# Late attention over two heads at a time, on two halves of TensorE's rows

## The chip, the core and the metric

One core of one Trainium2 chip runs the whole program. Its engines are TensorE (PE in the profile; PEld is its weight load), VectorE (DVE), ScalarE (ACT), GpSimd (POOL) and SyncE (SP, which here issues every DMA). The metric is the device time of one execution in microseconds (us). Times are compared by the median of several runs.

## The reference

Causal attention with a position bias over 4 batches, 8 heads, 576 positions and head size 64, then two feed-forward layers over the 2304 tokens. In short:

```python
scores = q @ k.T / sqrt(64) + minimum(-(cum[q] - cum[k]), 0)   # cum: running sum of max(s, 0); -1e9 where k > q
attn = softmax(scores);  x = attn @ v                          # the heads side by side: [2304, 512]
h = x @ w_in;   x = (h * clip(h + 3, 0, 6) / 6) @ w_out        # d_ff = 2048
h = x @ w2_in;  y = (h * tanh(softplus(h))) @ w2_out
```

All inputs are float32.

## The kernel before, in words

**Order.** Every step (a DMA, a group of matmuls, one DVE or ACT instruction) is a node with an engine, a cost and a priority. A planner (class `Plan`) runs the nodes through a list schedule when the program is built and writes each engine's instructions in that order. Buffers have tags with a fixed number of slots (`NBUF`), and the slots of a tag are handed out strictly in the order of the nodes' priorities (`turn`): a later user doesn't get a slot before an earlier one has taken his. PSUM has eight banks; late attention has banks 6 and 7, layer one's first matmul 4 and 5, its second 0 to 3.

**Precision.** Operands of the big matmuls are split in a high part (rounded to a shorter float32 format, "fp32r") and a low part (the rest). A product is made of high x high, high x low and low x high.

**Stages.** The queries of a batch are split at 256. *Early* attention (`small`, queries 0 to 255, two heads per call, scores in plain float32 on 64 rows of the array per head) runs first. *Late* attention (`unit`, queries 256 to 575 against all 576 keys) follows and lies among the matmuls of the first layer, since tokens are ordered so that blocks 0 and 1 need only early attention and blocks 2 to 4 the late one. Layer one takes five blocks of tokens (four of 512, one of 256) through 16 steps each: 12 matmuls into a hidden bank (L752), an activation, 12 matmuls with w_out into four banks (L785). At a block's end `y_out` copies the four banks to `st` buffers, ACT or DVE by choice of the planner, and the next block's first w_out matmul needs bank 0 empty. Layer two does the same with its own weights (L752, L790). Weights come in as 64-bit words and are turned into float32 by five DVE or ACT steps each (`load_split`).

**Late attention of one head** (`unit` before): q and k are loaded twice, once into each half of the 128 partitions (`qkr`), copied to the high part (`qk`), and the low parts are made (q's in `ql`, k's in partitions 64 to 127 of `qk`), so that one matmul on 128 rows gives q x (k high + k low). Three tiles of queries (128, 128 and 64) against 384, 512 and 576 keys give scores in banks (L493; the 576 in two halves of 288). DVE adds the bias and finds the row's extreme (L504), ACT takes the exponential (L515), the rows are scaled (L536, L538), PE transposes them 128 columns at a time (L548), ACT and DVE evict high and low part into `pt` (L279, L568), and ten matmuls with `v` (L586) give the head's output, which goes through an `st` buffer to memory (`xs`). A pair of heads shares one `st` buffer; its slot is taken with the first head's L586. `y_out` takes its slots from the same tag, and by priority block 0's come after those of the sixth pair of late attention.

Of the kernel before, what the change touches and what calls it, by code (L numbers as in the profile page):

```python
# [234 lines left out]
def tile_attention_moe_moe(ctx, tc, qk1, qk, v1, s, w_in, w_out, w2_in, w2_out, out):  # L235
    nc = tc.nc

    def r(ap):
# [181 lines left out]

    def unit(b, h, G, ta, tb, pair, prio, step, dep0, depc, banks, fi):
        q0, nk = P * ta, min(S, P * tb)
        nq = nk - q0
        nx = nq + nk
        c0 = COFF[ta]
        cn = (COFF[tb] if tb < 5 else CTOT) - c0
# [515 lines left out]
```

## Time and profile before

| | |
|---|---|
| median of 3 runs | 1042.32 us (1038.67 to 1042.41) |
| the profiled execution | 1043.16 us, its span from first to last instruction 1041.4 us |
| PE busy | 1008.0 us, 97% of the span |
| DVE, ACT, POOL busy | 636.7, 556.2 and 56.1 us |
| granted TensorE clock, mean | 0.981 of full speed |
| late scores (L493), first to last start | 119.6 to 474.9 us |

Matmuls are pipelined, so that a matmul's shown duration is longer than the time by which it delays the next; where this document gives the cost of a group on PE, it is the distance from its start to the next group's start.

### The profile page before, as it was taken

To read this page: it belongs to the slowest core of one execution; us is meant where nothing else is said; L and a number is where in the kernel's file an instruction comes from. 1 tells how busy PE (TensorE), PEld (TensorE's weight loads), DVE (VectorE), ACT (ScalarE), POOL (GpSimd) and SP (SyncE) were. 2 spreads that over 40 slices of the span, in tenths; PEclk is the share of its full clock that TensorE was granted. 3 is DMA by queue.
4 is the path that set the end of the run, shared out by engine and by line. 5 is a ranking of instruction groups with operands and counts; after the bars stand their busy time and mean duration, and the time that the engine had idled before them with its cause. 6 is when DMAs were issued, how large, how long until landed. Compare 5 with 4: busy or idle time off the path is not lost.

```text
span 1041.4 us, 14807 instructions
## 1 busy us (share of the span) xinstructions
PE 1008.0 (97%) x5064; PEld 821.7 (79%) x5064; DVE 636.7 (61%) x1519; ACT 556.2 (53%) x1172; POOL 56.1 (5%) x166
## 2 busy tenths in 40 slices
PE   6889999989999999999999999999999999999998
PEld 3456767867888889998888888888888898888886
DVE  6889999998897889996978999411111212111111
ACT  4878777776787778885435446322322323223222
POOL 2110111001001111000000000000000000000000
PEclk9869999989999999999999999999999999999999
DMA  7786876654645557543435545100100201001001
GB/s 234 232 259 217 310 245 220 213 163 164 219 155 194 163 196 241 198 134 124 154 125 172 172 164 192 59 1 21 41 1 1 81 1 61 1 1 41 1 0 41
DMA packets 60619, 135.63 MB, mean 130 GB/s; under 512 B 7072, under 2 KB 21440, under 8 KB 60544
## 3 DMA queue, kind: packets, MB, share of 16 engines
q1 hardware_dynamic: 60544, 134.69, 38.9%
q8 instruction: 40, 0.66, 0.3%
q14 instruction: 35, 0.29, 0.1%
HBM read 116.07 MB, written 18.59 MB: 129 GB/s over the span
## 4 chain that ended last, share of the span: by engine, by line
PE 82%; DVE 7%; DMA 6%; ACT 2%; issue 2%; SPq 0%; POOL 0%; DVEq 0%; ACTq 0%; POOLq 0%
PE b L752 34%; PE b L790 19%; PE b L785 15%; PE b L493 3%; PE b L548 3%; PE b L586 3%; DMA vr<-in_v_dram 2%; DMA wraw<-in_w_out_dram 2%; PE b L646 1%; PE b L702 1%; DVE cb L504 1%; PE b L693 1%; DVE wtmp L345 1%; DVE qk L444 1%; DMA wraw<-in_w_in_dram 1%
## 5 line engine op out<-in xcount | busy, mean ns | idle before, releaser
L752 PE MATMUL b<-blk,win 128*128 128x512 f32 (+1 forms) x1920 | 500.0, 373 | 2.6 <-DVE e L765 2.6
L752 PEld LDWEIGHTS b<-blk,win 128*128 128x128 f32 x1920 | 341.4, 189 | 67.0 <-DVE e L765 4.7
L785 PE MATMUL b<-g,wo 128*128 128x512 f32 (+1 forms) x960 | 255.4, 376 | 0.5 <-DVE wo L362 0.3
L785 PEld LDWEIGHTS b<-g,wo 128*128 128x128 f32 x960 | 167.2, 188 | 29.0 <-issue 0.8
L770 ACT ACTIVATE e<-b 128x512 f32<-128x512 f32 (+1 forms) x80 | 44.4, 555 | 258.0 <-PE b L752 257.7
L773 DVE TENSOR_TENSOR g<-e,g 128x512 fp32r<-128x512 f32 (+1 forms) x120 | 76.5, 638 | 167.4 <-ACT g L279 167.3
L790 PE MATMUL b<-wo,wo 128*128 128x512 f32 x432 | 121.1, 390 | 0.0
L790 PE MATMUL b<-wo,g 128*128 128x512 f32 x432 | 121.1, 390 | 0.0
L773 DVE TENSOR_TENSOR wo<-e,wo 128x512 fp32r<-128x512 f32 (+1 forms) x40 | 25.5, 638 | 148.2 <-ACT wo L279 148.0
L790 PEld LDWEIGHTS b<-wo,g 128*128 128x128 f32 x432 | 79.9, 188 | 15.5
L790 PEld LDWEIGHTS b<-wo,wo 128*128 128x128 f32 x432 | 79.8, 188 | 15.4
L279 ACT ACTIVATE g<-e 128x512 fp32r<-128x512 f32 (+1 forms) x107 | 63.4, 592 | 36.8 <-DVE e L765 20.1
L515 ACT ACTIVATE cb<-cb,nm 128x512 f32<-128x512 f32 (+2 forms) x96 | 66.9, 697 | 15.7 <-DVE nm L504 15.4
L279 ACT ACTIVATE pt<-b 128x512 fp32r<-128x512 f32 (+2 forms) x128 | 63.0, 497 | 17.0 <-PE b L548 9.6
L763 ACT ACTIVATE e<-b,three 128x512 f32<-128x512 f32 (+1 forms) x80 | 51.1, 639 | 20.5 <-PE b L752 17.6
L504 DVE CUSTOM_DVE_ANT_0 cb<-b,cb 128x512 f32<-128x512 f32 (+2 forms) x96 | 53.6, 562 | 9.3 <-PE b L493 5.9
L568 DVE TENSOR_TENSOR pt<-b,pt 128x320 fp32r<-128x320 f32 (+2 forms) x96 | 54.7, 573 | 4.6 <-ACT pt L279 4.0
L548 PEld LDWEIGHTS b<-ident,cb 128*128 128x128 f32 (+1 forms) x384 | 39.2, 140 | 21.3 <-issue 12.3
L548 PE MATMUL b<-ident,cb 128*128 128x128 f32 (+1 forms) x384 | 52.4, 258 | 2.9 <-DVE nm L504 1.1
L765 DVE SCALAR_TENSOR_TENSOR e<-e,b 128x512 f32<-128x512 f32 (+1 forms) x80 | 50.2, 627 | 2.1 <-ACT e L763 1.9
L586 PEld LDWEIGHTS b<-pt,v 128*128 128x128 f32 x320 | 47.1, 193 | 3.7 <-DVE pt L568 1.7
L369 DVE TENSOR_TENSOR wo<-wo 128x512 fp32r<-128x512 f32 x64 | 44.0, 687 | 8.8 <-ACT wo L279 8.5
(86 smaller groups left out, 1098.5 us busy)
## 6 DMA issues: line engine op xcount, KB each, us to landing
cb<-cuml SPq DMA_DIRECT2D x32, 736.0 KB, 4.5
wraw<-in_w_in_dram SPq DMA_DIRECT2D x32, 512.0 KB, 4.2
wraw<-in_w_out_dram SPq DMA_DIRECT2D x32, 512.0 KB, 4.0
wo<-wos SPq DMA_DIRECT2D x64, 256.0 KB, 3.0
qkr<-in_qk_dram SPq DMA_DIRECT2D x32, 448.0 KB, 3.5
vr<-in_v_dram SPq DMA_DIRECT2D x32, 160.0 KB, 2.5
cb<-cums SPq DMA_DIRECT2D x12, 384.0 KB, 4.8
qkr<-in_qk_dram SPq DMA_DIRECT2D x16, 256.0 KB, 3.1
```

The source lines that it names most:

```text
L279: nc.scalar.activation(out=out_, in_=in_, func=AF.Copy)
L504: nc.vector.tensor_tensor_reduce(out=p.t[0:n, g, o:o + w], in0=ps.t[0:n, z:z + w], in1=cb.t[0:n, g, o:o + w], scale=-0.125, scalar=(3.0e38 ...
L515: nc.scalar.activation(out=p.t[0:n, g, o:o + w], in_=p.t[0:n, g, o:o + w], func=AF.Exp, scale=-1.0, bias=nm.t[0:n, g, k:k + 1], accum_out= ...
L548: nc.tensor.transpose(out=ps.t[:, z:z + n], in_=p.t[0:n, g, o:o + P], identity=ident[0:n, 0:n])
L568: nc.vector.tensor_tensor(out=dl, in0=s_, in1=r(dh), op=ALU.subtract)
L586: nc.tensor.matmul(out=po.t[:, z + a:z + nq], lhsT=vt.t[:, g, c, :], rhs=pt.t[:, mt, g, f:f + nq - a], start=(j == 0), stop=(j == len(todo ...
L752: nc.tensor.matmul(out=hps.t[:, 0:N], lhsT=w.t[:, a, P * c:P * (c + 1)], rhs=x.t[:, c, b, :], start=(c == 0 and k == 0), stop=(c == NCC - ...
L763: a = add("ACT", actp(N, 1), lambda: nc.scalar.activation(out=e0.t[:, 0:N], in_=hps.t[:, 0:N], func=AF.Relu, bias=three, scale=1.0), [prev ...
L765: a = add("DVE", v1x(N), lambda: nc.vector.scalar_tensor_tensor(out=e0.t[:, 0:N], in0=e0.t[:, 0:N], scalar=6.0, in1=hps.t[:, 0:N], op0=ALU ...
L773: gl = add("DVE", v1x(N), lambda: nc.vector.tensor_tensor(out=g.t[:, 1, 0:N], in0=src.t[:, 0:N], in1=r(g.t[:, 0, 0:N]), op=ALU.subtract), ...
L785: nc.tensor.matmul(out=y[j].t[:, 0:N], lhsT=wt.t[:, a, P * j:P * (j + 1)], rhs=g.t[:, b, 0:N], start=(f == 0 and k == 0), stop=(f == NF - ...
L790: nc.tensor.matmul(out=y[j].t, lhsT=g.t[:, a, P * j:P * (j + 1)], rhs=wt.t[:, b, :], start=(f == 0 and k == 0), stop=(f == NF - 1 and k == 2),
```

## The change

`unit` works on two heads at a time. q and k of the pair are loaded once, head 0 in partitions 0 to 63 and head 1 in 64 to 127. The first two tiles of queries are scored per head on 64 rows of the array, three matmuls each (high x high, high x low, low x high), the heads alternating and each in its own bank; a job takes both attention banks at once, for which `can` now counts banks. The last 64 queries of both heads stand side by side as one tile of 128 (zeros fill the other head's rows), scored on all 128 rows and reduced, exponentiated and scaled together. Transposes are therefore all of 128 rows, in six groups per pair. Most buffers now hold a pair: `qk`, `qkr`, `cb`, `nm` and `l` have two slots, `v` and `pt` one. Early attention keeps its V and its transposed probabilities in a `qk` slot instead of `vr` and `pt`. The points at which transposes and products become due are moved.

```diff
     def can(self, n):
         need = {}
+        got = set()
         for b in n.new:
             if isinstance(b, Bank):
-                if not any(k in self.free_banks for k in b.banks):
+                k = next((k for k in b.banks if k in self.free_banks and k not in got), None)
+                if k is None:
                     return False
+                got.add(k)
...
-        "wo": 3, "qk": 2, "qkr": 2, "ql": 2, "cb": 3, "nm": 3, "l": 3, "v": 2, "vr": 1, "pt": 2,
+        "wo": 3, "qk": 2, "cb": 2, "nm": 2, "l": 2, "v": 1, "pt": 1, "qkr": 2,
...
+    def unit(b, h, prio, step, dep0, depc, banks):
+        ta, tb = 2, 5
...
+        nk0 = 3 * P
+        nx = nk0 + nk
...
-        raw = Buf(ap, "qkr", [P, G, nx], F32)
-        t = Buf(ap, "qk", [P, G, nx], F32R)
-        ql = Buf(ap, "ql", [P, G, nq], F32R)
-        cb = Buf(ap, "cb", [P, G, cn], F32)
+        raw = Buf(ap, "qkr", [P, nx], F32)
+        t = Buf(ap, "qk", [P, 2, nx], F32R)
+        cb = Buf(ap, "cb", [P, 2368], F32)
...
-        half, post = prio + 0.713 * step, prio + 1.539 * step
...
-        n_ql = A("DVE", v1x(G * nq), lambda: nc.vector.tensor_tensor(
-            out=ql.t, in0=raw.t[:, :, 0:nq], in1=r(t.t[:, :, 0:nq]), op=ALU.subtract), [n_h], pre, [ql], [raw, t])
-        n_kl = A("DVE", v1x(G * nk), lambda: nc.vector.tensor_tensor(
-            out=t.t[64:P, :, nq:], in0=raw.t[64:P, :, nq:], in1=r(t.t[64:P, :, nq:]), op=ALU.subtract), [n_h], pre, (), [raw, t])
...
+        half, post = prio + 1.0 * step, prio + 2.3 * step
+        n_ld = A("SP", 0.5, lambda: nc.sync.dma_start(out=raw.t, in_=qk[b, h // 2]), dep0, pre, [raw], lat=dma(P * nx * 4))
+
+        def ld_cb():
+            nc.sync.dma_start(out=cb.t[:, 0:1792].rearrange("p (g c) -> p g c", g=2),
+                              in_=cuml[row:row + 2, 0:896].rearrange("(o g) c -> o g c", o=1).to_broadcast([P, 2, 896]))
+            for g in range(2):
+                nc.sync.dma_start(out=cb.t[D * g:D * (g + 1), 1792:2368], in_=cuml[row + g:row + g + 1, 896:1472].to_broadcast([D, S]))
+        n_cb = A("SP", 1.0, ld_cb, depc, pre, [cb], lat=dma(P * 2368 * 4))
+        n_h = A(("ACT", "DVE"), (act(nx), v2x(nx)), lambda e: copy(e, t.t[:, 0, :], raw.t), [n_ld], pre, [t], [raw])
+        n_l = A("DVE", v1x(nx), lambda: nc.vector.tensor_tensor(
+            out=t.t[:, 1, :], in0=raw.t, in1=r(t.t)[:, 0, :], op=ALU.subtract), [n_h], pre, (), [raw, t])
...
+            for s_ in (slice(0, D), slice(D, P)):
+                nc.gpsimd.tensor_tensor(out=cb.t[s_, 2304:2368], in0=cb.t[s_, 2304:2368],
+                                        in1=cmask[s_, P + s_.start:P + s_.stop], op=ALU.add)
+        n_m = A("POOL", 0.9, mask, [n_cb], pre, (), [cb])
+
+        vt = Buf(ap, "v", [P, 2, tb, 2, D], F32R)
...
+        vr = Buf(ap, "qkr", [P, 2, tb, D], F32)
...
-            jobs = [[(i, 0, CW[i])] for i in range(ta, min(tb, 4))]
-            jobs += [[(4, 0, S // 2)], [(4, S // 2, S)]] if tb == 5 else []
-            last_m = None
-            for job in jobs:
-                ps = Bank(banks)
...
-                        for first, m in ((True, t), (False, ql)):
-                            nc.tensor.matmul(out=ps.t[0:n, z:z + e - a], lhsT=m.t[:, g, qo:qo + n], rhs=t.t[:, g, nq + a:nq + e],
-                                             start=first, stop=not first)
...
+        TERMS = ((0, 0), (0, 1), (1, 0))
...
+        for i, a, e in ((2, 0, 384), (3, 0, 512), (4, 0, 288), (4, 288, 576)):
+            w, qo, last = e - a, P * i - q0, e == CW[i]
+            ps = [Bank(banks)] if i == 4 else [Bank(banks), Bank(banks)]
+
+            def mm(ps=ps, i=i, a=a, e=e, w=w, qo=qo):
+                for k, (ka, kb) in enumerate(TERMS):
+                    for g in range(len(ps)):
+                        s_ = slice(0, P) if i == 4 else slice(D * g, D * (g + 1))
+                        nc.tensor.matmul(out=ps[g].t[:, 0:w], lhsT=t.t[s_, ka, qo:qo + P], rhs=t.t[s_, kb, nk0 + a:nk0 + e],
+                                         start=k == 0, stop=k == 2)
+            prev_s = A("PE", 3 * mm_cost(w), mm, [n_h, n_l, n_m, prev_s], prio, ps if prev_s else [*ps, nm, l], [t])
+            for g in range(len(ps)):
...
-        pt = Buf(ap, "pt", [P, 2, G, 1344], F32R)
+        pt = Buf(ap, "pt", [P, 2, 2, 1280], F32R)
...
-                        nc.tensor.transpose(out=ps.t[:, z:z + n], in_=p.t[0:n, g, o:o + P], identity=ident[0:n, 0:n])
-                        z += n
...
+            for g, cs in ([(0, (4, 3)), (0, (2, 1, 0))] if i == 4 else [(0, range(i, -1, -1)), (1, range(i, -1, -1))]):
                 ps = Bank(banks)
-                parts = [(c, i) for c in range(max(tiles) + 1) for i in tiles if c <= i]
-                parts.reverse()
-
-                def tr(ps=ps, parts=parts, g=g):
-                    z = 0
-                    for c, i in parts:
-                        n, o = min(P, S - P * i), COFF[i] - c0 + (P * c if c < 4 else S - P)
-                        nc.tensor.transpose(out=ps.t[:, z:z + n], in_=p.t[0:n, g, o:o + P], identity=ident[0:n, 0:n])
-                        z += n
-                prev_t = A("PE", sum(min(P, S - P * i) for _, i in parts) * 0.0008475, tr, n_n + [prev_t], half, [ps] if prev_t else [ps, pt], [p])
-
-                def views(ps, parts, g):
-                    i = parts[0][1]
-                    n, qo, nch = min(P, S - P * i), P * i - q0, len(parts)
+                nch = len(cs)
+
+                def tr(ps=ps, cs=cs, i=i, g=g):
+                    for z, c in enumerate(cs):
+                        o = off(i, g) + (P * c if c < 4 else S - P)
+                        nc.tensor.transpose(out=ps.t[:, P * z:P * (z + 1)], in_=p.t[:, o:o + P], identity=ident)
+                prev_t = A("PE", nch * P * 0.0008475, tr, [n_n[g], prev_t], half, [ps] if prev_t else [ps, pt], [p])
...
-        v = Buf(ap, "vr", [P, 2, 2, D], F32)
+        v = Buf(ap, "qk", [P, 4 * D + 768], F32)
...
-                unit(b, h, G, ta, tb, pair, prio + h * step, G * step, [n0], [nc0], banks, fi)
+                unit(b, h, prio + h * step, step, [n0], [nc0], banks)
...
-    qk = np.concatenate([qk, qk], axis=2)
+    qk = qk.reshape(NB, NH // 2, P, 320 + S)
+    tail = np.zeros((NB, NH // 2, 2, D, 2, D), np.float32)
+    for g in range(2):
+        tail[:, :, g, :, g] = qk[:, :, D * g:D * (g + 1), 256:320]
+    qk = np.concatenate([qk[..., :256], tail.reshape(NB, NH // 2, P, P), qk[..., 320:]], axis=3)
```

**PE, one unit's scores.** In the kernel before, the eight matmuls of one head, in a stretch where they stand close (b6, b7 are banks; `qk` holds the high q and both parts of k, `ql` the low q):

```order
L493 MATMUL b7_2488<-qk_2449 128x384
L493 MATMUL b7_2488<-qk_2449,ql_2469 128x384
L493 MATMUL b6_2499<-qk_2449 128x512
L493 MATMUL b6_2499<-qk_2449,ql_2469 128x512
...
L493 MATMUL b6_2513<-qk_2449 64x288
L493 MATMUL b6_2513<-qk_2449,ql_2469 64x288
...
L493 MATMUL b6_2527<-qk_2449 64x288
L493 MATMUL b6_2527<-qk_2449,ql_2469 64x288
```
In the changed kernel, the first pair's: the first three of six matmuls of 384 columns, which alternate between the banks, the first two of six of 512, and the two halves of the shared tile.

```order
L493 MATMUL b6_1480<-qk_1425 128x384
L493 MATMUL b7_1481<-qk_1425 128x384
L493 MATMUL b6_1480<-qk_1425 128x384
...
L493 MATMUL b6_1538<-qk_1425 128x512
L493 MATMUL b7_1539<-qk_1425 128x512
...
L493 MATMUL b6_1565<-qk_1425 128x288 x3
...
L493 MATMUL b7_1577<-qk_1425 128x288 x3
```
Sixteen matmuls per pair of heads have become eighteen, twelve of them on 64 rows.

**PE, ahead of block 1's first w_out matmul (into b0).** Before, one row from each group from the last main matmuls (L752, L785) on; L548 are transposes, L493 scores, L586 products with V:

```order
L752 MATMUL b5_2952<-blk_1370,win_626 128x512 x6
L548 MATMUL b6_2982<-ident_69,cb_2733 128x128 x3
L493 MATMUL b7_2987<-qk_2757 128x512
...
L752 MATMUL b5_2952<-blk_1370,win_626 128x512 x3
L548 MATMUL b7_3000<-ident_69,cb_2733 128x128 x4
L493 MATMUL b6_3005<-qk_2757 64x288
...
L548 MATMUL b6_3013<-ident_69,cb_2733 128x64 x5
L493 MATMUL b7_3024<-qk_2757 64x288
...
L586 MATMUL b6_3034<-pt_2983,v_2939 128x320 x6
...
L493 MATMUL b7_3053<-qk_2921 128x384
...
L785 MATMUL b0_3059<-g_2668,wo_2606 128x512 x3
```
Changed (L734 and L767 are the main matmuls, L539 transposes, L493 scores, L577 products):

```order
L734 MATMUL b5_2614<-blk_1231,win_580 128x512 x3
...
L539 MATMUL b7_2647<-ident_69,cb_2273 128x128 x4
...
L539 MATMUL b6_2668<-ident_69,cb_2273 128x128 x3
L577 MATMUL b7_2682<-pt_2622,v_2618 128x320 x6
...
L577 MATMUL b6_2694<-pt_2622,v_2618 128x320 x6
...
L493 MATMUL b6_2721<-qk_2465 128x512
...
L493 MATMUL b6_2748<-qk_2661 128x384
...
L493 MATMUL b6_2767<-qk_2661 128x512
...
L539 MATMUL b6_2785<-ident_69,cb_2493 128x128 x3
...
L539 MATMUL b7_2819<-ident_69,cb_2493 128x128 x3
...
L577 MATMUL b6_2839<-pt_2786,v_2708 128x320 x6
...
L767 MATMUL b0_2860<-g_2387,wo_2291 128x512 x3
```
Between the last L752 or L734 and the first w_out matmul into b0 stand two groups of transposes, four half scores, one head's products and a 384-wide score before; after the change it is ten groups of transposes, three score jobs of both heads, four halves of the shared tile and three heads' products. In both, eleven heads have had products by then.

**ACT, at block 0's output copies (`st` from b0, b1).** Before:

```order
L279 ACTIVATE pt_2983<-b6_2982 128x3x128
...
L279 ACTIVATE pt_2983<-b7_3000 128x4x128
...
L279 ACTIVATE pt_2983<-b6_3013 128x5x64
...
L808 ACTIVATE st_3046<-b0_1089 128x512
...
L808 ACTIVATE st_3057<-b1_1095 128x512
L593 ACTIVATE st_3035<-b6_3034 64x320
```
Changed (L282 is the copy that evicts transposes, L581 a head's output, L790 the output copy of a block):

```order
L282 ACTIVATE pt_2622<-b7_2647 128x4x128
...
L282 ACTIVATE pt_2622<-b6_2668 128x3x2x64
L581 ACTIVATE st_2683<-b7_2682 64x320
L581 ACTIVATE st_2683<-b6_2694 64x320
...
L282 ACTIVATE pt_2786<-b6_2785 128x3x128
...
L282 ACTIVATE pt_2786<-b7_2819 128x3x2x64
L790 ACTIVATE st_2851<-b0_1088 128x512
L790 ACTIVATE st_2854<-b1_1098 128x512
...
L581 ACTIVATE st_2840<-b6_2839 64x320
```
In both, the copy out of b0 stands behind the evictions of the sixth pair's transposes.

## Rows read from the trace of the kernel before

**Rows 1.** The page: the span, the engines' busy time, DVE over forty slices.
```profile
span 1041.4 us, 14807 instructions
...
PE 1008.0 (97%) x5064; PEld 821.7 (79%) x5064; DVE 636.7 (61%) x1519; ACT 556.2 (53%) x1172; POOL 56.1 (5%) x166
...
DVE  6889999998897889996978999411111212111111
```

**Rows 2.** Windows: busy us (and instructions) of each engine, PEclk, DMA share, GB/s.
```profile
78.00:234.00 156.00, 147.69 (x746) 111.59 (x746) 145.90 (x374) 121.23 (x276) 16.17 (x48) 0.98 0.68 229
...
286.00:468.00 182.00, 181.29 (x1173) 159.27 (x1172) 162.39 (x420) 146.80 (x314) 21.34 (x67) 1.00 0.56 183
```

**Rows 3.** Timeline of PE, 284 to 290 us: start, duration, line, tiles, count.
```profile
284.22 1.40 PE L586 MATMUL b<-pt,v 128*128 128x320 f32 x10
285.46 0.42 PE L493 MATMUL b<-qk 128*128 128x384 f32 x1
285.71 0.34 PE L493 MATMUL b<-qk,ql 128*128 128x384 f32 x1
285.89 0.85 PE L785 MATMUL b<-g,wo 128*128 128x512 f32 x3
...
287.95 0.49 PE L548 MATMUL b<-ident,cb 128*128 128x128 f32 x3
288.20 0.48 PE L493 MATMUL b<-qk 128*128 128x512 f32 x1
288.51 0.39 PE L493 MATMUL b<-qk,ql 128*128 128x512 f32 x1
288.74 0.86 PE L785 MATMUL b<-g,wo 128*128 128x512 f32 x3
```

**Rows 4.** Timeline of PE, 404 to 412 us.
```profile
406.04 0.52 PE L752 MATMUL b<-blk,win 128*128 128x256 f32 x3
406.40 0.60 PE L548 MATMUL b<-ident,cb 128*128 128x128 f32 x4
406.75 0.61 PE L785 MATMUL b<-g,wo 128*128 128x256 f32 x3
407.20 0.87 PE L752 MATMUL b<-blk,win 128*128 128x256 f32 x6
408.00 0.52 PE L548 MATMUL b<-ident,cb 64*128 64x64 f32 x5
408.45 0.62 PE L752 MATMUL b<-blk,win 128*128 128x256 f32 x3
...
409.63 0.29 PE L493 MATMUL b<-qk 128*64 128x288 f32 x1
409.76 0.30 PE L493 MATMUL b<-qk,ql 128*64 128x288 f32 x1
```

**Rows 5.** Timeline of PE, 30 to 35 us: early scores on 64 rows.
```profile
30.87 0.93 PE L646 MATMUL b<-qkr 64*128 64x128 f32 x8
...
33.16 0.92 PE L646 MATMUL b<-qkr 64*128 64x128 f32 x4
```

**Rows 6.** DVE, groups by form: count, busy us, mean ns, idle before.
```profile
L444 DVE TENSOR_TENSOR qk<-qkr,qk 64x576 fp32r<-64x576 f32 x32 | 24.2, 756 | 0.4
...
L504 DVE CUSTOM_DVE_ANT_0 cb<-b,cb,nm 64x288 f32<-64x288 f32 x32 | 16.2, 507 | 7.0 <-PE b L493 5.8 <-issue 0.6 <-DVE nm L504 0.2
...
L442 DVE TENSOR_TENSOR ql<-qkr,qk 128x320 fp32r<-128x320 f32 x32 | 15.5, 484 | 2.4 <-ACT qk L279 2.2
...
L504 DVE CUSTOM_DVE_ANT_0 cb<-b,cb 64x288 f32<-64x288 f32 x32 | 14.3, 446 | 2.9 <-PE b L493 2.9
```

**Rows 7.** Timeline of PE, 256 to 266 us.
```profile
257.72 0.66 PE L548 MATMUL b<-ident,cb 128*128 128x128 f32 x4 [0.20 <-DVE nm L504]
...
261.02 2.66 PE L586 MATMUL b<-pt,v 128*128 128x320 f32 x10 [0.60 <-DVE pt L568]
...
264.27 1.58 PE L785 MATMUL b<-g,wo 128*128 128x512 f32 x6
```

More of the change, by code (lines that the diff above doesn't have):

```diff
@@ L460, in half_v @@
-        def half_v(e, g, low):
-            h0 = D * ((h + g + low) % 2)
-            return vt.t[:, g, :, h0:h0 + D]
-        def v_h(e):
-            for g in range(G):
-                copy(e, half_v(e, g, 0), vr.t[:, g])
-        def v_l():
-            for g in range(G):
-                nc.vector.tensor_tensor(out=half_v(None, g, 1), in0=vr.t[:, g], in1=r(half_v(None, g, 0)), op=ALU.subtract)
+            for s_ in (slice(0, D), slice(D, P)):
+                nc.gpsimd.tensor_tensor(out=cb.t[s_, 2304:2368], in0=cb.t[s_, 2304:2368],
+                                        in1=cmask[s_, P + s_.start:P + s_.stop], op=ALU.add)
@@ L471, in unit, with v_view @@
+        n_m = A("POOL", 0.9, mask, [n_cb], pre, (), [cb])
+        vt = Buf(ap, "v", [P, 2, tb, 2, D], F32R)
+        def v_view(low):
+            return vt.t[:, :, :, low, :]
+        vr = Buf(ap, "qkr", [P, 2, tb, D], F32)
         n_v0 = A("SP", 0.5, lambda: nc.sync.dma_start(
-            out=vr.t, in_=v1[b, h:h + G, :, 0:tb, :].rearrange("g p c d -> p g c d")), dep0, prio, [vr], lat=dma(P * G * tb * D * 4))
-        n_v1 = A(("ACT", "DVE"), (G * act(tb * D), G * v1x(tb * D)), v_h, [n_v0], prio=post, new=[vt], uses=[vr])
@@ new lines, in unit, with norm, views @@
+        n_p = []
+        for i in range(ta, tb):
+            n_n = {}
+            for g in range(1 if i == 4 else 2):
+                def norm(eng, o=off(i, g), k=col(i, g), w=CW[i]):
+                    v = p.t[:, o:o + w]
+                    if eng == "ACT":
+                        nc.scalar.activation(out=v, in_=v, func=AF.Copy, scale=l.t[:, k:k + 1])
+                    else:
+                        nc.vector.tensor_scalar(out=v, in0=v, scalar1=l.t[:, k:k + 1], scalar2=None, op0=ALU.mult)
+                n_n[g] = A(("DVE", "ACT"), (0.06 + v2x(CW[i]), act(CW[i], 1)), norm, [n_r], half, (), [p, l])
+            for g, cs in ([(0, (4, 3)), (0, (2, 1, 0))] if i == 4 else [(0, range(i, -1, -1)), (1, range(i, -1, -1))]):
+                ps = Bank(banks)
+                nch = len(cs)
[4 more added lines that the diff above has]
+                prev_t = A("PE", nch * P * 0.0008475, tr, [n_n[g], prev_t], half, [ps] if prev_t else [ps, pt], [p])
+                def views(ps, cs, i, g):
+                    nch = len(cs)
@@ L555, in views @@
                     if i == 4:
[L556 to L563 removed]
+                        s_ = ps.t[:, 0:nch * P].rearrange("p (c g n) -> p c g n", g=2, n=D)
@@ L599, in unit @@
[L599 to L606 removed]
+                n_ph = A("ACT", actp(nch * P), ev_h, [prev_t], half, (), [ps, pt])
@@ new lines, in unit, with pv @@
+                n_pl = A("DVE", v1x(nch * P), ev_l, [n_ph], half, (), [ps, pt])
+                n_p += [n_ph, n_pl]
+        x = Buf(main_p, "st", [P, 512], F32)
+        n_x, n_pv = [], None
+        for g in range(2):
+            po = Bank(banks)
+            hi, lo = (0, D) if g == 0 else (D, 0)
+            def pv(po=po, g=g):
+                for c in range(tb):
+                    a = max(0, P * c - q0)
+                    f = (3 - c) * nq + a if c < 4 else 0
+                    w = vt.t[:, g, c].rearrange("p a d -> p (a d)")
+                    for k in range(2):
+                        nc.tensor.matmul(out=po.t[:, a:nq], lhsT=w, rhs=pt.t[:, k, g, f:f + nq - a],
+                                         start=c == 0 and k == 0, stop=c == tb - 1 and k == 1)
+            n_pv = A("PE", 0.2 + 2 * sum(mm_cost(nq - max(0, P * c - q0)) for c in range(tb)), pv, n_p + [n_v1, n_v2, n_pv], post,
+                     [po] if g else [po, x], [po, pt, vt])
+            n_b = A("ACT", actp(nq), lambda po=po, hi=hi, lo=lo: nc.scalar.activation(
+                out=x.t[hi:hi + D, 0:nq], in_=po.t[lo:lo + D, 0:nq], func=AF.Copy), [n_pv], post, (), [po, x])
+            n_x.append(A("DVE", v1x(nq), lambda po=po, hi=hi: nc.vector.tensor_tensor(
+                out=x.t[hi:hi + D, 0:nq], in0=po.t[hi:hi + D, 0:nq], in1=x.t[hi:hi + D, 0:nq], op=ALU.add),
+                [n_b], post, (), [po, x]))
```

174 lines of the change are left out of this document (56 added, 118 removed).

## The prediction

> **What bounds the kernel now.** I read the engines' busy line first, then the same by stage, then single stretches of TensorE's timeline. TensorE (PE) is busy 97% of the span and VectorE (DVE) 61%, but DVE's slices stand at 8 or 9 tenths for the first twenty-odd of forty and at 1 to 2 behind them [rows 1]. Two stages matter. From 78 to 234 us both are full: PE 147.69 and DVE 145.90 of 156 us, 94%. From 286 to 468 us PE is busy 181.29 of 182 us and DVE 162.39 [rows 2], so there PE alone sets the pace and a microsecond of PE work removed is a microsecond of time. Late attention lies in both, about 5.5 of its 16 pairs of heads ahead of 264 us (eleven of 32 heads have had their last product by then) and 10.5 behind it. From 468 us on no attention is left, only the two layers' matmuls, which the change does not touch.
>
> **What a pair costs PE now.** A duration here is the distance from a group's start to the next group's start. One head's scores: the 384-wide job 285.46 to 285.89, 0.43 us; the 512-wide one 288.20 to 288.74, 0.54 [rows 3]; the two 288-wide jobs are two matmuls each, 0.13 apart (409.63 to 409.76), 0.52 [rows 4]. That is 1.49. Its transposes: three of 128 take 0.25 (287.95 to 288.20) [rows 3], four 0.35, five of 64 rows 0.45 (408.00 to 408.45). The last group costs something ahead of it too: six 256-wide matmuls before it take 0.80 (407.20 to 408.00) where three elsewhere take 0.36 (406.04 to 406.40), so six would take 0.72, and 0.08 is the entry into 64 rows [rows 4]. Together 1.13. The products with V, ten matmuls in 1.24 (284.22 to 285.46) [rows 3], keep their number and widths. A pair without them: 2 x (1.49 + 1.13) = 5.24 us.
>
> **What it costs after.** In the 384- and 512-wide jobs each head now has three matmuls on 64 rows (high x high, high x low, low x high) in place of two on 128, and the two heads alternate between rows 0 to 63 and 64 to 127, into two banks. Whether the two halves run side by side decides the change. The trace has the case: the early attention's scores use 64 rows per head, one head behind the other. Four matmuls of one head take 0.92 us, and eight, of two heads whose turns met, 0.93 [rows 5]. So I count a round of two as one. A second matmul of a job shows its bare length: 0.18 for 384 (285.71 to 285.89), 0.23 for 512 [rows 3]. Three rounds of each are 0.54 and 0.69. The 64 last queries of both heads share a 128-row job of three matmuls per half, six of 0.13, 0.78. Two visits to 64 rows cost 0.08 in and, as an estimate from that row, as much out: 0.32. Scores: 2.33. Transposes are now all of 128 rows, in groups of 3, 3, 4, 4, 2, 3: 3 x 0.25 + 2 x 0.35 + 0.17 = 1.62. Sum 3.95, so **a pair saves 1.29 us of PE**, 20.6 over sixteen. If the halves did not overlap, 0.54 + 0.69 would come on top and 0.06 would be left.
>
> The Trainium skill (TensorEngine Tiling (Array Packing), Key Properties) speaks against the change here: changing the tiling mode drains TensorE. The row agrees that a change costs, 0.08 at the entry. Counted by the rule alone, as two new visits per pair with nothing taken away, 16 x 0.32 = 5.1 us would be lost; the sum above already holds them, and it also drops the two 64-row visits that the 64-query transposes made.
>
> **The late stage.** 10.5 x 1.29 = 13.5 us less, straight off the time, since PE has no gap to absorb it.
>
> **The early stage.** Here DVE counts as well. Per pair the four subtractions that make the low parts (2 x 0.484 + 2 x 0.756 = 2.48 us) become one of 960 columns; the slope between those rows, 0.272 us over 256 columns, gives 1.16 for it, so 1.32 less. One head's two 288-wide reductions go, 0.507 + 0.446 = 0.95 [rows 6]. Together 2.27 per pair, 12.5 over 5.5. ScalarE gets less to do in the same way (one 960-wide copy for two of 896, one 576-wide exponential for two). If DVE sets the pace up to 264 us the gain is 12.5, if PE does 5.5 x 1.29 = 7.1. I take 10.
>
> Against it stands **one hold**. The first w_out matmul of block 1 needs bank 0, which block 0's output copy empties, and that copy takes an st buffer only after the sixth pair of late attention has taken its own. So PE has nothing but attention to do until then. Now: transposes from 257.72, block 1's first w_out matmul at 264.27 [rows 7], 6.55 us for some 3.2 us of work at full pace (0.35 + 0.52 + 0.53 + 1.24 + 0.43, with the durations above, and some 0.1), so 3.4 us lost. After, the stretch between the same two points holds far more, since the late pairs start later (they share two bias and two q/k buffers with the early ones) and one pair is in hand at a time: ten groups of transposes (2.7), scores of 512, 384 and 512 in both heads and four halves of 288 (4.0), three products (3.7), 10.4 us. At the present ratio, 6.55 / 3.2, that takes 21.3 us and loses 10.9, so 7.5 more than now. The bounds: nothing lost in it (3.4 better than now), or twice as much, 18 more. The work in it isn't extra, it comes from before and behind.
>
> Net early: -10 + 7.5 = -2.5. **The sum**: 1043.16 (the profiled execution, 1041.4 us of span and 1.8 around it; the runs' median is 1042.32) - 13.5 - 2.5 = **1027**. Hidden: POOL's added work on the mask and the two more DMA issues per pair, since POOL is busy 5% [rows 1] and the q/k load and bias load of a pair are issued some twelve steps ahead; uncovered, a late mask would hold a pair's first scores and with them the matmuls behind it in PE's queue.
>
> **Rivals.**
> - *The early stage gives more.* DVE's 12.5 us come through whole and the hold loses no more than now or nothing: -13.5 - 12.5 and up to -3.4: 1014 to 1017; with somewhat smoother main matmuls 1008. For it: DVE at 94%. Against: PE is as full. Chance 0.17.
> - *No overlap of the halves.* Late 0.6, early the DVE part alone against the hold: 1040. Against it stand the two rows of 0.93 and 0.92 [rows 5]; for it, that those are matmuls in another format. 0.05.
> - *The hold takes back all that the early stage gives and more*, 18 in place of 7.5: 1038 to 1042. 0.11.
> - *Slower: pairs queue up behind one another.* There is one pt and one v buffer where there were two, and a score job takes both attention banks at once. A pair's first transposes wait until the last pair's twenty products have run, and its scores until both banks are emptied, by two engines in turn; PE takes its instructions in order, so main matmuls wait behind. If every pair behind 264 us met a hold like today's, 3.4 us [rows 7], that is 36 us: 1063; the point from which it decides is 16 / 10.5 = 1.5 us per pair. For it: the single buffers. Against: two to three groups of main matmuls of 0.7 us stand between most attention groups in the new order, and PE now waits only 0.7 us in the whole stage [rows 2] with the same two banks. 0.12.
>
> The forecast itself has 0.55, with a range of its own from 1018 to 1036. The range that leaves out no more than two in ten reaches into the rivals on both sides: 1008 to 1042. What a measurement of this kernel can tell from no change is about 0.5%, 5 us. Faster, below 1037: 0.55 + 0.17 + a part of the hold's and of the no-overlap case, 0.76. Same 0.11, slower 0.13.
>
> **What would show it.** A 384-wide score job of both heads takes 0.55 to 0.75 us from its first start to the next group's (1.2 if the halves don't overlap), a 512-wide one 0.7 to 0.9. Transposes come in groups of 0.25 and 0.35 with no 64-row group. From 286 us to the end of attention PE stays above 98% busy (below 95% is the queueing rival). One stretch of some 20 us without a main matmul stands ahead of block 1's first w_out matmul (over 30 is the hold rival), and that matmul starts near 262 us. DVE's total falls by some 36 us, 16 x 2.27. The forecast is wrong if the overlap fails, or if the new order leaves holds that this one reading doesn't count.

## The result and the profile after

The changed kernel takes 1057.93 us (median of 4 runs, 1056.42 to 1058.98), the kernel before, measured beside it, 1042.37: ratio 1.0144, 95% interval 1.0118 to 1.0169. It is 15.6 us slower; 16 us faster was forecast. The page of after, against [rows 1]: TensorE (PE) is busy 5.5 us more in a span 15.1 us longer, VectorE (DVE) 31.8 us less, and a dip in the clock row stands at the tenth and eleventh slices.

```profile
span 1056.5 us, 14136 instructions
...
PE 1013.5 (96%) x5016; PEld 816.8 (77%) x5016; DVE 604.9 (57%) x1373; ACT 511.9 (48%) x1078; POOL 46.3 (4%) x102
...
DVE  6788989976677776876877999611111212111111
...
PEclk9659999997899998999999999999999999999999
```

Windows of after (columns as in [rows 2]), and below them two of before. In the late stage PE now stands idle 10.07 of 210 us, where it stood idle 0.71. From 234 to 286 us it is idle 8.78 us and its granted clock is 0.80, against 1.55 us and 0.97.

```profile
78.00:234.00 156.00, 151.90 (x786) 113.51 (x785) 140.73 (x340) 111.65 (x256) 17.67 (x30) 0.99 0.69 216
234.00:286.00 52.00, 43.22 (x209) 33.09 (x207) 33.54 (x78) 32.10 (x67) 4.30 (x12) 0.80 0.52 141
...
290.00:500.00 210.00, 199.93 (x1245) 171.04 (x1244) 154.47 (x359) 129.22 (x275) 11.50 (x32) 0.98 0.46 133
```

```profile
234.00:286.00 52.00, 50.45 (x276) 40.97 (x275) 43.31 (x109) 38.33 (x80) 5.81 (x19) 0.97 0.57 192
...
290.00:500.00 210.00, 209.29 (x1318) 182.65 (x1317) 179.87 (x450) 161.73 (x343) 20.30 (x63) 1.00 0.53 173
```

PE's timeline of after, against [rows 3, 7]. A pair's 384-wide scores (x6, both heads) take 0.72 to 0.73 us to the next start, its 512-wide ones 0.89, three transposes 0.25: the halves overlap. From 242.92 to 272.38 us no main matmul runs, 29.5 us. Within it groups wait for the ScalarE and VectorE step between them, 7.2 us in all, and from 254.5 us on the work goes at half the pace: three 288-wide scores take 0.89 us (269.98 to 270.87) where they take 0.39 at 292.15. The granted clock is 0.50 there, the lower of PE's two levels (1.2 GHz); it fell after PE had stood idle between groups. Over the whole stretch it is 0.65, where it was 0.75 in the stretch of before (windows, the first line after, the second before).

```profile
242.92:272.38 29.46, 22.22 (x93) 16.01 (x92) 17.38 (x42) 17.01 (x36) 1.52 (x4) 0.65 0.47 121
257.72:264.27 6.55, 5.20 (x25) 4.44 (x26) 4.64 (x13) 5.71 (x13) 0.00 (x0) 0.75 0.62 200
```

```profile
240.18 0.49 PE L539 MATMUL b<-ident,cb 128*128 128x128 f32 x3
240.43 1.63 PE L734 MATMUL b<-blk,win 128*128 128x512 f32 x6
...
242.92 1.30 PE L539 MATMUL b<-ident,cb 128*128 128x128 f32 x8
...
247.41 4.51 PE L577 MATMUL b<-pt,v 128*128 128x320 f32 x20 [1.24 <-DVE pt L560]
...
254.90 3.85 PE L493 MATMUL b<-qk 128*128 128x288 f32 x12 [0.90 <-DVE nm L500]
...
269.98 1.09 PE L493 MATMUL b<-qk 128*128 128x288 f32 x3 [0.37 <-DVE pt L560]
270.87 1.68 PE L577 MATMUL b<-pt,v 128*128 128x320 f32 x10
272.38 0.94 PE L767 MATMUL b<-g,wo 128*128 128x512 f32 x3
...
286.09 0.80 PE L493 MATMUL b<-qk 64*128 64x384 f32 x6
286.82 0.96 PE L767 MATMUL b<-g,wo 128*128 128x512 f32 x3
...
289.09 0.96 PE L493 MATMUL b<-qk 64*128 64x512 f32 x6
289.98 0.96 PE L767 MATMUL b<-g,wo 128*128 128x512 f32 x3
...
292.15 0.55 PE L493 MATMUL b<-qk 128*128 128x288 f32 x3
292.54 1.40 PE L577 MATMUL b<-pt,v 128*128 128x320 f32 x10
```

The chain that ended last, in order of time (start, us, what), 336 to 457 us of after: seven transfers of 256 KB each stand on it, 39.7 us together. Before, the chain has none between 300 and 460 us.

```profile
336.90 4.11 DMA wo<-wos
355.64 5.04 DMA wo<-wos
380.04 7.05 DMA blk<-xs
396.24 2.62 DMA wo<-wos
400.03 8.29 DMA ys<-st
428.52 6.46 DMA wo<-wos
450.85 6.12 DMA wo<-wos
```

The issue list of after gives such a w_out load a median of 2.7 us, and the larger of a pair's three bias loads 6.8. SP issues pairs' bias loads at 333.12, 351.39, 378.47, 396.95, 426.78 and 446.75 us: each of the six longer transfers above is issued within 5 us behind one, the only short one (396.24) ahead of one. The same holds for all 256 KB transfers of w_out, block and y from 290 to 500 us: the 12 that are issued while a bias load is under way take 6.71 us in the median, the 28 others 2.67. Before it was 3.63 against 2.74. A pair's bias is 1184 KB, less than the 1472 KB that its two heads loaded before; what grew is the single load.

```profile
wo<-wos SPq DMA_DIRECT2D x64, 256.0 KB, 2.7
cb<-cuml SPq DMA_DIRECT2D x16, 896.0 KB, 6.8
```

### The profile page after: what moved, and what is told of

It reads as the page before. It is cut to its first block, busy times and chain, and to the rows that moved or that the text cites. A ratio compares the mean times of both kernels' runs of the same rounds, so it can differ in the third digit from the quotient of the medians.

```text
span 1056.5 us, 14136 instructions
## 1 busy us (share of the span) xinstructions
PE 1013.5 (96%) x5016; PEld 816.8 (77%) x5016; DVE 604.9 (57%) x1373; ACT 511.9 (48%) x1078; POOL 46.3 (4%) x102
## 4 chain that ended last, share of the span: by engine, by line
PE 67%; DMA 5%; DVE 1%; ACT 1%; issue 0%; SPq 0%; ACTq 0%
PE b L734 31%; PE b L772 19%; PE b L767 13%; DMA wo<-wos 3%; PE b L539 2%; PE b L493 2%; DMA ys<-st 1%; PE b L577 1%; DMA blk<-xs 1%; ACT st L790 0%; ACT cb L508 0%; ACT cb L528 0%; DVE pt L560 0%; DVE st L583 0%; DVE cb L530 0%
## 5 line engine op out<-in xcount | busy, mean ns | idle before, releaser
L734 PE MATMUL b<-blk,win 128*128 128x512 f32 (+1 forms) x1920 | 503.0, 375 | 0.6 <-ACT st L282 0.5
L734 PEld LDWEIGHTS b<-blk,win 128*128 128x128 f32 x1920 | 343.2, 190 | 68.3 <-issue 4.4
L767 PE MATMUL b<-g,wo 128*128 128x512 f32 (+1 forms) x960 | 261.6, 382 | 5.5 <-ACT st L790 5.1
L767 PEld LDWEIGHTS b<-g,wo 128*128 128x128 f32 x960 | 166.6, 191 | 39.1 <-issue 8.2
L752 ACT ACTIVATE e<-b 128x512 f32<-128x512 f32 (+1 forms) x80 | 44.4, 555 | 262.5 <-PE b L734 260.2
L772 PEld LDWEIGHTS b<-wo,wo 128*128 128x128 f32 x432 | 79.5, 188 | 15.1
L282 ACT ACTIVATE g<-e 128x512 fp32r<-128x512 f32 (+1 forms) x99 | 58.9, 595 | 41.4 <-PE b L767 37.5
L508 ACT ACTIVATE cb<-cb,nm 128x384 f32<-128x384 f32 (+2 forms) x80 | 54.5, 682 | 30.8 <-DVE nm L500 30.7
L560 DVE TENSOR_TENSOR pt<-b,pt 128x384 fp32r<-128x384 f32 (+2 forms) x96 | 54.1, 574 | 11.8 <-ACT pt L282 11.0
L493 PE MATMUL b<-qk 64*128 64x384 f32 (+2 forms) x288 | 53.2, 393 | 5.7 <-DVE nm L500 2.8
L539 PE MATMUL b<-ident,cb 128*128 128x128 f32 x304 | 51.5, 284 | 7.2 <-issue 2.8
L282 ACT ACTIVATE pt<-b 128x384 fp32r<-128x384 f32 (+2 forms) x96 | 47.9, 503 | 17.6 <-PE b L539 17.1
L539 PEld LDWEIGHTS b<-ident,cb 128*128 128x128 f32 x304 | 37.8, 145 | 22.8 <-issue 10.6
L500 DVE CUSTOM_DVE_ANT_0 cb<-b,cb 128x384 f32<-128x384 f32 (+2 forms) x80 | 44.9, 585 | 13.6 <-PE b L493 10.2
L577 PEld LDWEIGHTS b<-pt,v 128*128 128x128 f32 x320 | 48.0, 196 | 3.8 <-ACT pt L282 1.4
```

What stands on the lines that cost most here:

```text
L282: nc.scalar.activation(out=out_, in_=in_, func=AF.Copy)
L493: nc.tensor.matmul(out=ps[g].t[:, 0:w], lhsT=t.t[s_, ka, qo:qo + P], rhs=t.t[s_, kb, nk0 + a:nk0 + e], start=k == 0, stop=k == 2)
L508: nc.scalar.activation(out=p.t[:, o:o + w], in_=p.t[:, o:o + w], func=AF.Exp, scale=-1.0, bias=nm.t[:, k:k + 1], accum_out=l.t[:, k:k + 1],)
L539: nc.tensor.transpose(out=ps.t[:, P * z:P * (z + 1)], in_=p.t[:, o:o + P], identity=ident)
L560: nc.vector.tensor_tensor(out=dl, in0=s_, in1=r(dh), op=ALU.subtract)
L577: nc.tensor.matmul(out=po.t[:, a:nq], lhsT=w, rhs=pt.t[:, k, g, f:f + nq - a], start=c == 0 and k == 0, stop=c == tb - 1 and k == 1)
```

## Where the time went, stage by stage

The main matmuls (weights `win` or `wo`) stream the same columns in every kernel here, so the moments at which they have streamed 196,608, 245,760 and 540,672 columns, read from their starts in the trace, cut a run into three stages. The stage between the first two holds the stretch without main matmuls; the longest gap between the starts of two main matmuls is given, and its place. Ratios are to the kernel before measured beside each (its medians go from 1041.88 to 1045.17 us), with 95% intervals; the stages are of the one profiled execution. Run 4, with the loads and the order of after, has a third stage 5.6 us shorter than after: some 6 us of a stage can come without any change of loads or order.

| kernel | median us | ratio | to 196,608 | to 245,760 | to 540,672 | longest gap (at) | PE idle, 290 to 500 |
|---|---|---|---|---|---|---|---|
| before | 1042.37 | 1 | 223.1 | 50.4 | 217.1 | 7.2 (257) | 0.7 |
| after | 1057.93 | 1.0144 (1.0118, 1.0169) | 214.6 | 68.1 | 222.9 | 29.7 (243) | 10.1 |
| 1 copies of y first | 1058.29 | 1.0129 (1.0077, 1.0182) | 216.0 | 43.7 | 244.8 | 14.8 (482) | 14.5 |
| 2 before, copies first | 1050.57 | 1.0059 (1.0029, 1.0090) | 226.1 | 41.5 | 230.3 | 4.9 (408) | 6.2 |
| 3 bias by POOL's queue | 1091.01 | 1.0451 (1.0392, 1.0511) | 230.5 | 67.6 | 238.9 | 33.3 (256) | 20.7 |
| 4 heads in turn | 1054.03 | 1.0105 (1.0069, 1.0140) | 216.0 | 68.6 | 217.3 | 31.4 (244) | 6.5 |
| 5 after, bias once | 1039.62 | 0.9972 (0.9951, 0.9993) | 215.6 | 67.7 | 206.9 | 32.1 (243) | 0.8 |
| 6 before, bias once | 1041.88 | 0.9988 (0.9967, 1.0010) | 223.9 | 48.0 | 216.9 | 5.7 (256) | 0.6 |
| 7 three bias slots | 1048.50 | 1.0072 (1.0039, 1.0106) | 222.1 | 58.5 | 214.8 | 22.8 (248) | 6.7 |
| 8 bias in parts | 1048.68 | 1.0062 (1.0037, 1.0087) | 218.4 | 63.8 | 220.1 | 28.1 (246) | 6.3 |
| 9 once, copies first | 1045.18 | 0.9985 (0.9955, 1.0015) | 213.5 | 41.1 | 236.6 | 15.5 (468) | 11.2 |
| 10 parts, copies first | 1044.60 | 0.9994 (0.9968, 1.0021) | 212.7 | 42.4 | 235.8 | 12.2 (471) | 10.5 |
| 11 parts, copies a little ahead | 1042.91 | 0.9989 (0.9965, 1.0014) | 213.8 | 63.0 | 211.5 | 20.2 (249) | 3.9 |
| 12 parts, three slots | 1052.41 | 1.0065 (1.0031, 1.0098) | 218.7 | 66.0 | 214.3 | 32.6 (244) | 6.0 |
| 13 two pt buffers | 1059.08 | 1.0139 (1.0095, 1.0183) | 220.1 | 69.3 | 220.4 | 31.6 (248) | 8.4 |
| 14 once, copies a little ahead | 1042.68 | 0.9977 (0.9952, 1.0002) | 213.5 | 65.7 | 209.7 | 20.0 (253) | 1.5 |
| 15 as 11, attention due earlier | 1045.75 | 1.0024 (0.9994, 1.0055) | 222.4 | 57.6 | 211.8 | 20.8 (251) | 3.4 |
| 16 bias by ScalarE's queue | 1081.65 | 1.0366 (1.0328, 1.0405) | 223.0 | 72.4 | 237.3 | 36.0 (250) | 18.7 |
| 17 as 11, by ScalarE's queue | 1059.76 | 1.0155 (1.0087, 1.0222) | 225.9 | 65.9 | 219.7 | 19.4 (266) | 7.6 |

After against before: -8.5, +17.7 and +5.8, together +15.0. Two theories were put up first: the stretch, from the rank of the output copies (run 1), and the bias loads, behind which small transfers come late (run 3). The rival of the second was the prediction's own, pairs that queue for the single pt and v buffers and the two banks.

## The experiments

**1 and 2. The stretch, moved.** The copies of block outputs take their st buffers ahead of the attention's (in 2, the kernel before, `prio - 13`).

```diff
             t = Buf(main_p, "st", [P, 512], F32)
+            t.key = prio - (12 if i == 0 else 18)
```

> The changed kernel with one line more: the st buffers of a block's output copies in layer one rank ahead of the fifth pair's (block 0) and ahead of the twelfth pair's (block 1), so that no stretch of the order holds attention alone. Theory 'hold': the stretch without a main matmul ahead of block 1's first w_out matmul, 29.5 us against 6.55 before, is why the early gain is lost; without it 14 to 18 us come back, 1041 to 1045. Rival 'the work only moves': the attention left over is met later behind other waits, and the time stays at 1054 or more.

> The kernel before with the same rank for its output copies (13 priority units earlier). Theory 'hold': its own stretch loses only 3.4 us, so at most 1 to 4 us come back, 1038 to 1042. Rival: the rank of the copies matters for any kernel here, and it gains as much as the changed one, 1030 or less.

The stretch is gone and 24.4 us with it, but the next stage is 21.9 us longer: the attention put off there comes due later, and a stretch of 14.8 us without main matmuls stands at 482 us. It ends with the fourth block's first w_out matmul: the same hold, at a later border (run 9 below shows its copies). Nothing is won; before loses by the same edit.

**3, 16 and 17. The bias loads on another queue.** `nc.sync.dma_start` becomes `nc.gpsimd.dma_start` (3) or `nc.scalar.dma_start` (16, 17) for the three loads of `cb`.

> The changed kernel with the three bias loads of a pair issued by POOL instead of SP; nothing else moved by hand. Theory 'bias burst': behind 290 us the waits of 1 to 2 us come from w_out and block loads that land late (5 to 8 us against 3) behind a pair's 1.2 MB of bias in SP's queue; then those landings go back to about 3 us and the late stage gets 6 to 9 us shorter, 1049 to 1053, with the hold as it is. Rival 'pairs queue up': the waits come from the single pt and v buffers and the scores' two banks, and the time stays within 3 us of 1058.

> The changed kernel with the bias loads, whole and with two slots as they are, issued from ScalarE's queue, so that w_out, block and y loads on SP's queue do not stand behind them. Computes the reference. If the small loads behind a bias load are what PE waits for late (chain of 4 to 8 us loads from 336 to 451 us), those rows go, PE's idle time from 290 to 500 us falls below 4 us, and the time is 1040 to 1050 us. If the refill of the two slots is, the rows change places and the time stays within 5 us of 1058. ScalarE waits in its own order for a slot to come free, which can cost a few us by itself.

> The bias in three buffers, copies of y 3 units ahead, and the bias loads issued from ScalarE's queue. Computes the reference. If the queue order still costs something beside parts (PE idle 3.9 us from 290 to 500 us in that kernel): 1036 to 1041 us, the first version below both kernels. If parts and little else was the cure: within 3 us of 1043.

Each is slower than the same kernel with its bias on SP's queue (17 than run 11) and than any of its forecasts, though the planner's order moved too, so that the loss itself isn't explained. The chain of run 16 shows that the queue isn't the point: small transfers, on SP's queue without the bias loads now, still take 7 to 8 us while a bias load is under way (14 of them, 7.33 us in the median; the 27 others 2.71).

```profile
393.87 8.03 DMA blk<-xs
...
421.75 7.29 DMA ys<-st
448.48 7.87 DMA wo<-wos
474.44 7.38 DMA wo<-wos
```

The Trainium skill (DMA: Bandwidth & Descriptors, Issuing engines are not separate DMA queues) says that transfers from all queues run on the same 16 engines and interleave; these rows agree.

**4. Is it the alternation that makes the halves overlap?** The loops over heads and terms change places, so that one head's three matmuls stand ahead of the other's.

```diff
-                for k, (ka, kb) in enumerate(TERMS):
-                    for g in range(len(ps)):
+                for g in range(len(ps)):
+                    for k, (ka, kb) in enumerate(TERMS):
```

> The changed kernel with the three matmuls of head 0 ahead of the three of head 1 in the 64-row score jobs (384 and 512 columns), in place of alternating. If the halves of the rows overlap only where neighbours differ, a 384-wide job goes from 0.72 to 1.1 or more, and 16 x 1.2 us come on top at most, 1065 to 1077; if the engine pulls the second head's matmuls ahead by itself, as the early scores' eight in 0.93 us suggest, the time stays within 3 us of 1058.

It isn't: six of 512 still take 0.91 us to the next start, against 0.89. (The time, 1054.03 us, is a little below the forecast's band; the intervals of the two ratios overlap.)

```profile
292.18 0.97 PE L493 MATMUL b<-qk 64*128 64x512 f32 x6
293.09 0.96 PE L767 MATMUL b<-g,wo 128*128 128x512 f32 x3
```

**5 and 6. The bias loads, taken away** from both kernels, in the order of each.

```diff
+            if not bias0:
+                bias0.append(ap().pool.tile([P, 2368], F32, tag="bias0", name="bias0", bufs=1))
...
+            nc.sync.dma_start(out=cb.t[:, 0:16], in_=cuml[row:row + 1, 0:16].to_broadcast([P, 16]))
...
-                        out=p.t[:, o:o + w], in0=pb.t[:, 0:w], in1=cb.t[:, o:o + w], scale=-0.125,
+                        out=p.t[:, o:o + w], in0=pb.t[:, 0:w], in1=bias0[0][:, o:o + w], scale=-0.125,
```

> The changed kernel in the same order on every engine, but the bias row of the first pair is loaded once and added for every late pair; what is left of each pair's three bias loads is one of 16 columns. The low parts of the probabilities overwrite the high parts in the pair's buffer, which makes room for the one bias tile. So it leaves out the other pairs' biases, their masks and the high parts. Theory (the pair's bias load of 1.2 MB is what holds up the pairs: its slot is refilled in about 7 us, and what is loaded behind it comes late): the time falls by 20 us or more, to 1025 to 1038 us, and is 5 to 15 us below that of the kernel before treated in the same way. Rival (the work inside a pair is too long a chain, with one pt, one v and two banks, whatever is loaded): it stays within 6 us of 1058, and 8 to 20 us above the kernel before treated in the same way.

> The kernel before with the same treatment as the run on the bias loaded once: one bias tile for all late heads, a load of 16 columns in place of each head's 736 KB, low parts over high parts. It leaves out the other heads' biases, masks and the high parts. Theory (a head's 4.5 us load with three slots was nearly hidden before): 1030 to 1042 us, so that the changed kernel without its bias loads is the faster of the two by 5 to 15 us. Rival (chain inside the pair): within 4 us of 1042, and the changed kernel stays slower by 8 to 20 us.

The changed kernel falls by 18 us (a little short of the 20 that the theory named), before by one or none. Windows of run 5: the late stage is full again (0.78 us idle), the stretch is as it was (7.71 us idle, clock 0.74).

```profile
234.00:286.00 52.00, 44.29 (x207) 34.55 (x207) 33.11 (x77) 31.80 (x67) 2.41 (x12) 0.74 0.28 84
...
290.00:500.00 210.00, 209.22 (x1315) 180.16 (x1314) 165.94 (x381) 136.03 (x286) 5.90 (x28) 1.00 0.34 103
```

So the two losses are apart: the late one is the bias loads, the stretch isn't. Of the chain's seven transfers two are left, of 3.58 and 3.96 us. The run leaves out the masks with the biases, but POOL still fills the same places, and no step of POOL stands on the chain of after. The probabilities' high parts are left out too; run 13 leaves them out with the loads whole and gains nothing. Single pt, single v and two banks per job are as in after, and PE no longer waits: none of them is the late loss.

**7, 12 and 13. Slots.** In 7 `"cb": 3`, in 13 `"pt": 2`; room comes from one edit.

```diff
-        pt = Buf(ap, "pt", [P, 2, 2, 1280], F32R)
+        pt = Buf(ap, "pt", [P, 1, 2, 1280], F32R)
```

> The changed kernel with three bias slots of a pair in place of two; room for it comes from the probabilities' buffer, in which the low parts overwrite the high ones (it leaves out the high parts in the product with V). All bias loads are whole. If what counts is that a pair's slot is refilled only after the pair's last transpose: 1040 to 1050 us, with PE's waits in the late stage halved. If what counts is that the small loads come late behind 1.2 MB: within 4 us of 1058, and the loads of w_out, ys and blk still take 4 to 8 us to land.

> The changed kernel with two buffers for a pair's transposed probabilities in place of one; the low parts overwrite the high ones in each to make room (it leaves out the high parts). The rival put on record ahead of the result names the single pt buffer as what pairs queue for: then 1040 to 1050 us. If they queue for the bias buffers, a second pt buffer does nothing: within 4 us of 1058.

> The changed kernel with the bias in three buffers and three slots of each in place of two, the low parts of the probabilities over the high ones to make room (it leaves out the high parts). If the slots and the size of one load are two causes, they add up and the bias loads cost as good as nothing: within 4 us of the 1039.6 of the run without bias loads. If they are one cause, the time stays at 1046 to 1050 as with either alone.

A third bias slot gives some 7.5 us back (1.0144 to 1.0072), a second pt buffer nothing: the single pt buffer, which the prediction named, is no cause. Slots and parts together (run 12) give no more than either. The slot's refill isn't what the late stage of after waits for: from 286 us on, a pair's last bias load lands 8 to 17 us ahead of its first scores. Run 5 keeps the two slots, and SP's wait for them is 11.9 us from 290 to 470 us where it was 13.2. In run 7 the chain still holds seven such transfers of 3.4 to 6.9 us; what its third slot gave isn't shown, the planner's order moved with it.

**8, 10 and 11. The bias in parts.** Each head's bias, and the shared rows', has a buffer, a load and a mask of its own, in the same memory; 10 adds the ranking of run 1, 11 `prio - 3` in its place.

```diff
+        cb = [Buf(ap, "cb", [P, 896], F32), Buf(ap, "cb", [P, 896], F32), Buf(ap, "ct", [P, S], F32)]
...
+        n_cb = [A("SP", 0.5, lambda g=g: nc.sync.dma_start(
+            out=cb[g].t, in_=cuml[row + g:row + g + 1, 0:896].to_broadcast([P, 896])), depc, pre, [cb[g]], lat=dma(P * 896 * 4)) for g in range(2)]
```

> The changed kernel whose pair's bias is held in three buffers, one of each head (448 KB) and one of the shared last rows (288 KB), in the same memory as before: each is loaded, masked and given free by itself. Computes the reference. Theory (bias load and its slots): each part is back 10 us earlier and no load stands behind more than 0.45 MB; 1038 to 1050 us, 8 to 20 us below the changed kernel. Rival (chain inside the pair): 1054 to 1062 us.

> The changed kernel with the bias in three buffers, each loaded, masked and given free by itself, and the copies of y ranked ahead. Computes the reference. If the losses are apart: 1034 to 1044 us. If the stretch's work only moves: 1046 to 1052, with a stretch of no main matmuls past 370 us.

> As the kernel with the bias in three buffers, with the copies of y ranked only 3 units ahead of the attention's outputs, which moves the first of them alone. Computes the reference. It has nearly the long stretch at 243 to 270 us still: if that stretch sets the time, within 4 us of 1048.7; if the order late in the attention counts more, 1038 to 1045.

Parts give back 8 to 9 us, and the small transfers issued behind a part take 3.67 us in the median (run 8) where they took 6.71; the order moved here too, more than in run 7. Runs 10 and 11 reach the kernel before and don't pass it.

**9, 14 and 15. Both losses at once, and an earlier start.** Runs 9 and 14 are run 5 with the rankings of 1 and 11. Run 15 is run 11 with `[-20, 1, 12, ...]` for the windows' starts.

> The changed kernel with the bias row loaded once (the other pairs' biases, masks and the probabilities' high parts are left out, as in that run) and with the copies of y ranked ahead of the attention's outputs, which took the stretch without main matmuls at 243 to 272 us away. If the two losses are apart (about 18 us from the bias loads, about 13 us from the stretch), they add up: 1024 to 1033 us. If the work of that stretch only moves to a later place, as it did with the loads in, the time stays within 4 us of 1039.6.

> The changed kernel with the bias row loaded once (the other pairs' biases, masks and the high parts are left out) and the copies of y ranked 3 units ahead, which in the kernel with three bias buffers cut the stretch without main matmuls from 28 to 20 us and moved none of it to the end of the attention. If stretch and bias loads are the whole loss against the forecast, taking away the loads and 8 us of the stretch gives 1029 to 1034; if the stretch's 8 us turn up elsewhere, 1038 to 1042.

> The kernel with the bias in three buffers and the copies 3 units ahead, with the late attention's first two windows due earlier: the starts 2 and 20 become 1 and 12, their lengths 22 and 35.07 become 22.66 and 37.88. Computes the reference. If the attention as a whole is what comes late, an earlier start gives some of it back: 1034 to 1040; if the stretch ahead of block 1's first w_out matmul stays at 20 us and sets the time, within 3 us of 1042.9.

All three miss their better number. In run 9 the stretch is gone from 243 us and stands at 468: PE's timeline there shows the last pair's transposes and products waiting one by one for DVE, with no main matmul between them.

```profile
469.55 0.64 PE L495 MATMUL b<-qk 128*128 128x288 f32 x3
...
475.56 1.72 PE L541 MATMUL b<-ident,cb 128*128 128x128 f32 x8 [0.99 <-DVE pt L562]
...
480.76 2.66 PE L579 MATMUL b<-pt,v 128*128 128x320 f32 x10 [1.17 <-DVE pt L562]
483.24 1.63 PE L769 MATMUL b<-g,wo 128*128 128x512 f32 x3
```

That matmul is the fourth block's first with w_out. The third block's output copies stand in ScalarE's order behind the last pair's evictions, as block 0's did in after:

```profile
479.63 0.49 ACT L282 ACTIVATE pt<-b 128x384 fp32r<-128x384 f32 x1 [0.62 <-PE b L541]
...
480.53 0.92 ACT L793 ACTIVATE st<-b 128x256 f32<-128x256 f32 x3
```

So runs 1, 9 and 10 move the hold to a later border (it stands at 482, 468 and 471 us, each time ahead of this matmul) and don't take it away. In run 14 the stretch is cut in two, 7.8 us at 241 and 20.0 at 253, and hardly shortened; in run 15 the stage ahead of it grew by more than it gained (8.6 against 5.4 us, beside run 11).

## Why the prediction was wrong, by its own steps

- **The pair's cost** was nearly right: 0.72 + 0.89 + 2 x 0.39 for the scores, 1.59 for the transposes (3 x 0.25 + 2 x 0.35 + 0.14), 3.98 against 3.95. The cost before was 0.15 too high: start to start over all its late groups, scores and transposes take 5.09 a pair, not 5.24. The same mean in run 5 is 4.09, so a pair saves 1.0 us, not 1.29. The two 64-row jobs cost 0.18 and 0.20 above three bare rounds, 0.38 a pair where 0.32 was allowed. The Trainium skill (TensorEngine Tiling (Array Packing), Key Properties) says that a change of tiling mode drains TensorE; these rows agree that a visit costs, and don't show how much of it is the drain.
- **The early term**, -10, measured -8.5 at 196,608 columns. DVE's total fell 31.8, not 36.
- **The late term**, -13.5, came out as +5.8: this is the step that failed most. The words "straight off the time, since PE has no gap to absorb it" took a stage without waits as one that can have none. Without bias loads the term is -10.0 (206.9 against 216.9), about 10.5 x 1.0; the loads cost 16.0 (222.9 against 206.9). The step behind it is the one that called the loads hidden because they are "issued some twelve steps ahead". A pair's bias is indeed there in time, 8 to 17 us ahead of its first scores; what was put at nothing is what its bytes do to others. A pair's loads are 1.2 MB in one go where a head's was 736 KB, and while they run, 256 KB transfers for the main matmuls take 4 to 8 us.
- **The hold**, +7.5, was mis-sized: by its own terms it came to 29.5 - 10.4 - 3.4 = +15.7, near the bound of 18 that the text gave, and the stage that holds it grew by 17.7. Its 10.4 us of work were scaled by the ratio of before, 2.05; the ratio was 29.5 / 10.4 = 2.8. Both parts of it rose: PE idle per us of work from 0.42 to 0.70 (1.35 of 3.2, 7.24 of 10.4), and the pace fell with the granted clock, 0.75 before and 0.65 after. The place and the cause (copies behind the attention's outputs) were as read: run 1 takes the stretch away.
- **The rivals.** PE did come to wait in the late stage, so the side of the last rival (slower) was right. Its mechanism, pairs that queue for the single pt and v and for both banks, was wrong: a second pt buffer does nothing (run 13), and with v and the banks as they are PE doesn't wait once the bias loads are gone (run 5). PE's busy share from 290 to 500 us is 95.2%, just above the mark that was set for it.
- **Two slips without weight.** Attention doesn't end at 468 us in the kernel before: late scores start up to 474.9. And the 1040 of the no-overlap rival goes with 10 us for the early stage; with the 12.5 that it names it is 1038.

**What stays open.** With the bias loads gone or in parts, and the stretch whole, moved or cut in two, the main matmuls reach 540,672 columns at 488 to 491 us (runs 5, 9, 10, 11, 14), where the kernel before does at 490.6. No run is without both losses: 5 has the whole stretch, 9 and 10 have it at a later border, 11 and 14 keep 20 us of it. So it isn't shown that the change would win if both were gone. That the pair, as one long piece for ScalarE and DVE, needs cover that the order doesn't have is what run 9's rows suggest; it wasn't shown by taking that chain apart. Why slots and parts each give back about half of what run 5 does is open too, since both edits move the planner's order.

## What to carry to other kernels

When two units of work are joined, their loads join too: cost the larger transfer by what the small, urgent ones beside it will take, not by its issue, and try it in parts. A stage that shows no waits has cover for the waits of its present order only. When a hold goes from one place, look for it at the next place of the same kind before calling it cured. Saved matmul time came through where other matmuls stood between the dependent steps (10.0 us in run 5's late stage); where attention stood alone (the 29.5 us of after), TensorE waited and its granted clock was 0.65.

## What was not expected

- Two heads' scores on the two halves of the array overlap whichever way they are written, as the early scores had hinted: 0.89 us alternating, 0.91 in turn, for six of 512.
- Bias loads on a second hardware queue didn't free the first: the larger ones still land in 6.9 us there, small transfers on SP's queue beside them take 7 to 8, and the kernel, its order moved by the edit too, is 2.2% slower than the changed one (1.0366 against 1.0144).
